# A kernel whose order is written out as numbers: new tables for every engine's order, the dummy products and the PSUM banks

## The chip, the cores and the metric

The kernel runs on one core of a Trainium2 chip. The metric is the device time in microseconds (us) of one execution. Five engines of the core work side by side, each through its own list of instructions in order: TensorE (PE, matrix products; its weight loads are listed as PEld), VectorE (DVE), ScalarE (ACT), GpSimd (POOL) and SyncE (SP, which only issues DMA transfers). They wait for each other by semaphores. Products land in PSUM, which has eight banks.

## The reference

Two parts follow each other: linear attention with second-order features, and a gated feed-forward network on its result.

```python
def phi(x):                       # per head: 32 numbers -> 8 x 8 features
    a = np.einsum('rd,bhsd->bhsr', S1, x)
    b = np.einsum('rd,bhsd->bhsr', S2, x)
    return np.einsum('bhsi,bhsj->bhsij', a, b).reshape(*x.shape[:-1], r * r)
q_p, k_p = (phi(q), phi(k))       # 4 batches, 4 heads, 1088 positions, r = 8
kv = np.einsum('bhsf,bhsd->bhfd', k_p, v)
z = np.sum(k_p, axis=2)
num = np.einsum('bhsf,bhfd->bhsd', q_p, kv)
den = np.einsum('bhsf,bhf->bhs', q_p, z)[..., None] + 1e-06
x = (num / den)                   # heads joined: 4352 tokens x 128
gate = np.maximum(x @ w_gate, 0.0)          # 128 x 1536
return gate * (x @ w_val) @ w_out           # 1536 x 128
```

## The kernel before, in words

**Stages.** For each batch b the keys are loaded, transposed on VectorE (kt1), multiplied by the sketches on TensorE (ksk) and transposed back out of PSUM by VectorE (kt2). From that come z (TensorE), its scaled copy (zc), a product that puts z beside the sketch weights (w, wc), the key features (kphi: POOL, for batch 0 partly VectorE from a PSUM copy kbc that ScalarE makes) and the sum of features times V (kv on TensorE, kve on VectorE). V is cast to FP16 by ScalarE (vc). Queries go the same way: qt1, qsk, qt2, then bw, red, rd and an for the denominator, qphi for the features, a transpose (qtr, qpt), and num and x, which write a column block of x, transposed, to SBUF.

The first 512 tokens of batch 0 have a path of their own to be ready early (class First, names that begin with f): f sk and f t2 for the scores, f aT, f aTe and f csk for the denominator, f bw, f red and f rd (reciprocal), f rx, f rT and f rTe to spread it, f phi (POOL), f tr and f pt for the features, f num and f xd for the result, each for two halves 0 and 1. The second 512 tokens of batch 0 are group "0,4", which goes the way of the others.

**Feed-forward units.** 102 units follow on x. A unit is a block of tokens by a block of w_gate and w_val columns: g and v are the two products (512 columns of PSUM each), relu (ScalarE) evicts g, h (VectorE) multiplies it by v out of PSUM, and o multiplies by w_out, accumulating in a bank over all units of one token block. In 19 units ScalarE copies v out (vcp) and POOL multiplies (hp). oe evicts the sum, st stores it. Units 0 to 5 belong to the first 256 tokens, 6 to 11 to the next, 12 to 23 to group "0,4". Within a token block the first third of the units uses the first third of the weights (wg0, wv0, wo0), and so on.

**Loads.** SP issues most loads in this order: S1 and S2, the second part of k (k01), V of batch 0 in eight pieces (v000 to v013), wo0, wg0, wv0 as raw float32 (ScalarE casts them: cw), q01, and then k, q and v of the later batches. ScalarE issues the first parts of k and q. POOL issues the other weights (wv1, wg2, wg1, wv2, wo1, wo2) as casting transfers, and in between an instruction named gate: a memset of one element of the buffer that k of batch 1 goes to, so that k1 and all that stands behind it on SP waits for POOL to reach it.

**What sets the order.** Each operation is registered with its engine, its name and what it reads. The table START holds a number for each of the 857 operations; they are issued in the order of these numbers, so that the numbers of one engine's operations are that engine's order. BANKS holds, for each of 268 uses of PSUM, the bank or pair of banks. WARM says ahead of which operation how many dummy products are issued: products of a zero tile with itself, into bank 7, that nothing reads. A chain list (RINGS) orders some operations of different engines when the tables are made; it doesn't change.

```python
order = sorted(self.ops, key=lambda o: (START[o.seq] if START else 0, o.seq))
for o in order:
    if o.seq in WARM:
        warm(WARM[o.seq])
    o.fn()
```

Lines of the profile that the text uses: L1015 dummy products, L367 st (the sketches by an identity), L370 ws, L375 wq, L484 and L486 kt1 of batch 0, L491 kt1 of the others, L507 kt2, L537 kbc, L543 kphi, L557 and L561 vc, L310 weight loads by POOL, L316 cw, L385 L, L391 gate, L394 loads of k, L626 f rx, L624 f rd, L631 f rTe, L532 wc, L641 f pt, L695 f phi, L715 f xd, L987 qt1, L793 qt2, L807 red, L811 rd, L916 g and v, L921 relu, L931 h, L944 o.

Of the kernel before, what the change touches and what calls it, by code (L numbers as in the profile page):

```python
# [32 lines left out]
    2, 5, 0, 8, 4, 42, 10, 11, 12, 16, 18, 23, 25, 29, 3, 13, 1, 14, 33, 68, 36, 87, 20, 98, 71,  # L33
    52, 110, 66, 88, 119, 6, 9, 15, 7, 19, 26, 21, 22, 49, 56, 93, 96, 125, 137, 120, 156, 100,
    105, 113, 190, 171, 132, 221, 207, 396, 446, 441, 451, 387, 17, 28, 31, 34, 35, 41, 47, 51,
    74, 79, 39, 50, 40, 44, 54, 72, 46, 32, 53, 73, 80, 81, 83, 85, 90, 163, 160, 170, 178, 191,
    194, 209, 213, 199, 210, 279, 185, 259, 254, 292, 296, 299, 302, 306, 214, 196, 229, 233,
    265, 270, 309, 314, 367, 383, 358, 438, 291, 324, 450, 455, 459, 460, 463, 298, 289, 312,
    320, 364, 373, 429, 433, 540, 577, 345, 473, 509, 516, 594, 599, 605, 608, 612, 27, 24, 30,
    37, 43, 48, 55, 59, 61, 63, 64, 69, 77, 58, 62, 38, 45, 60, 65, 67, 70, 76, 86, 91, 57, 78,  # L40
    82, 92, 97, 75, 89, 94, 109, 117, 84, 95, 102, 99, 108, 104, 106, 112, 115, 129, 157, 198,
    203, 212, 216, 126, 131, 140, 144, 147, 161, 164, 169, 172, 189, 183, 215, 228, 223, 234,
    240, 243, 246, 250, 269, 319, 322, 238, 252, 260, 288, 294, 318, 362, 369, 315, 308, 321,
    326, 332, 354, 363, 372, 378, 401, 420, 470, 479, 395, 405, 412, 418, 454, 475, 522, 530,
    434, 449, 478, 488, 482, 494, 507, 513, 533, 550, 568, 626, 630, 529, 547, 601, 637, 642,
    658, 703, 706, 506, 514, 511, 538, 598, 602, 606, 610, 621, 742, 749, 103, 114, 136, 142,
    176, 122, 128, 149, 154, 184, 101, 107, 116, 123, 200, 111, 121, 118, 135, 205, 152, 158,
    159, 168, 220, 146, 162, 155, 174, 222, 231, 335, 310, 305, 313, 124, 134, 127, 148, 235,
    138, 167, 166, 175, 217, 239, 141, 153, 143, 150, 173, 245, 133, 145, 130, 139, 165, 257,
    151, 177, 193, 197, 226, 258, 195, 206, 204, 218, 261, 268, 287, 284, 295, 301, 232, 241,  # L50
    266, 276, 293, 219, 224, 242, 247, 304, 272, 297, 290, 307, 317, 331, 278, 282, 280, 303,
    323, 337, 273, 277, 274, 283, 349, 300, 316, 256, 264, 333, 351, 375, 458, 381, 436, 592,
    181, 187, 188, 201, 249, 179, 182, 202, 208, 263, 180, 192, 253, 262, 275, 225, 236, 251,
    271, 281, 227, 230, 237, 255, 285, 186, 211, 244, 248, 267, 286, 311, 390, 330, 486, 340,
    328, 336, 344, 352, 385, 327, 341, 343, 348, 393, 342, 350, 353, 359, 394, 347, 356, 380,
    384, 398, 355, 361, 370, 376, 411, 325, 329, 334, 339, 416, 368, 379, 400, 407, 422, 374,
    386, 414, 419, 426, 440, 338, 346, 357, 366, 444, 360, 365, 371, 392, 445, 388, 403, 410,
    415, 447, 408, 413, 423, 428, 464, 469, 582, 671, 490, 596, 404, 409, 402, 421, 489, 431,
    437, 468, 471, 492, 432, 443, 427, 456, 493, 417, 424, 472, 477, 497, 425, 430, 406, 442,
    501, 382, 391, 389, 399, 505, 435, 453, 462, 467, 510, 466, 474, 452, 461, 508, 526, 481,  # L60
    485, 377, 397, 498, 531, 457, 465, 499, 503, 544, 519, 525, 517, 534, 552, 476, 480, 439,
    448, 520, 557, 580, 733, 587, 679, 684, 495, 500, 512, 518, 559, 484, 496, 532, 541, 561,
    483, 491, 502, 523, 564, 487, 504, 524, 528, 572, 539, 551, 562, 566, 578, 537, 546, 543,
    553, 581, 535, 542, 527, 536, 567, 589, 549, 556, 565, 573, 614, 515, 521, 554, 558, 616,
    555, 570, 574, 579, 632, 600, 607, 609, 615, 634, 569, 584, 624, 631, 643, 649, 813, 804,
    676, 741, 548, 560, 576, 585, 651, 545, 563, 583, 591, 654, 603, 613, 611, 620, 655, 586,
    590, 622, 625, 656, 593, 597, 618, 623, 628, 662, 633, 639, 648, 652, 673, 619, 627, 663,
    666, 677, 571, 575, 595, 604, 681, 588, 617, 636, 641, 687, 629, 635, 638, 647, 692, 640,
# [984 lines left out]
```

## Time and profile before

| what | value |
|---|---|
| runs | 101.98, 315.89, 101.86 us; median 101.98 |
| span of the profiled execution (first to last instruction) | 100.1 us |
| instructions | 3180 |
| DMA | 14799 packets, 12.40 MB |
| products of g and v (L916) | 264 |
| products of o (L944) | 408 |
| dummy products (L1015) | 55, busy 5.9 us |
| relu (L921) | 102, 56.3 us busy, 613 ns mean |
| h (L931) | 84, 53.5 us busy, 673 ns mean |
| hp (L936) | 19, 21.7 us busy, 1158 ns mean |

The profiled execution has no time of its own beside its span; the runs' median lies 1.9 us above that span, which holds what comes before the first and after the last instruction. One of the three runs took 315.89 us; it is an outlier, and the median is not affected.

How to read the rows: a row of the timeline is start, duration (both us), engine, line, operation, what is written and read, how many instructions are merged, and in brackets how long the engine had been idle and for what it waited. A row of the stages is from:to, length, then busy time and (count) for PE, PEld, DVE, ACT and POOL, then the granted clock of TensorE, the share of the 16 DMA engines and GB/s. A row of the chain is start, duration, engine and line. SPq is the queue of SP. Ends of matrix products are modelled.

### The profile page before, as it was taken

To read this page: it belongs to the slowest core of one execution; us is meant where nothing else is said; L and a number is where in the kernel's file an instruction comes from. 1 tells how busy PE (TensorE), PEld (TensorE's weight loads), DVE (VectorE), ACT (ScalarE), POOL (GpSimd) and SP (SyncE) were. 2 spreads that over 40 slices of the span, in tenths; PEclk is the share of its full clock that TensorE was granted. 3 is DMA by queue.
4 is the path that set the end of the run, shared out by engine and by line. 5 is a ranking of instruction groups with operands and counts; after the bars stand their busy time and mean duration, and the time that the engine had idled before them with its cause. 6 is when DMAs were issued, how large, how long until landed. Compare 5 with 4: busy or idle time off the path is not lost.

```text
span 100.1 us, 3180 instructions
## 1 busy us (share of the span) xinstructions
PE 94.2 (94%) x1223; PEld 68.3 (68%) x1223; DVE 82.7 (83%) x175; ACT 84.1 (84%) x169; POOL 65.8 (66%) x89
## 2 busy tenths in 40 slices
PE   6999989989999999999999999999999999999950
PEld 6978969848779965557673656765676665688940
DVE  4778779999989998999998689799746879897940
ACT  3445889999799798998999999899999999998730
POOL 6029947898988999999897699935944404001700
PEclk9999999999999999999999999999999999999999
DMA  2988889999930525208664200071217305003331
GB/s 43 370 229 267 146 122 358 339 269 276 342 125 0 111 66 134 45 12 235 165 182 99 60 0 7 1 169 27 52 29 120 78 0 129 2 7 84 99 105 52
DMA packets 14799, 12.40 MB, mean 124 GB/s; under 512 B 8256, under 2 KB 12352, under 8 KB 14784
## 3 DMA queue, kind: packets, MB, share of 16 engines
q1 hardware_dynamic: 13392, 10.70, 38.5%
q0 software_dynamic: 864, 0.79, 5.8%
q10 hardware_dynamic: 528, 0.72, 2.2%
q8 instruction: 9, 0.15, 0.7%
q14 instruction: 6, 0.05, 0.2%
HBM read 9.05 MB, written 2.23 MB: 113 GB/s over the span
## 4 chain that ended last, share of the span: by engine, by line
PE 81%; ACT 6%; POOL 4%; DMA 3%; issue 1%; DVE 1%
PE ps L916 42%; PE ps L944 23%; PE ps L1015 5%; ACT g_sb L921 4%; DMA wg<-in_moe_w_gate_dram 3%; PE ps L848 3%; PE ps L501 2%; PE ps L780 2%; POOL kp L543 2%; PE ps L567 2%; ACT v_sb L925 1%; POOL fqp L695 1%; ACT qpt L840 1%; PE ps L515 1%; POOL wv L310 1%
## 5 line engine op out<-in xcount | busy, mean ns | idle before, releaser
L921 ACT ACTIVATE g_sb<-ps 128x512 f16<-128x512 f32 x102 | 56.3, 613 | 3.9 <-PE ps L916 3.2
L931 DVE TENSOR_TENSOR ht<-g_sb,ps 128x512 f16<-128x512 f16 (+1 forms) x84 | 53.5, 673 | 7.2 <-PE ps L916 5.6
L916 PE MATMUL ps<-xT,wv 128*128 128x512 f16 (+1 forms) x132 | 35.6, 332 | 0.5 <-ACT g_sb L921 0.5
L916 PE MATMUL ps<-xT,wg 128*128 128x512 f16 (+1 forms) x132 | 34.3, 332 | 0.3 <-DMA wg<-in_moe_w_gate_dram 0.3
L944 PEld LDWEIGHTS <-ht 128*128 128x128 f16 x408 | 28.0, 98 | 9.2 <-issue 0.8
L944 PE MATMUL ps<-wo,ht 128*128 128x128 f16 x408 | 33.8, 219 | 0.0
L936 POOL TENSOR_TENSOR ht<-g_sb,v_sb 128x512 f16<-128x512 f16 x19 | 21.7, 1158 | 16.4 <-ACT g_sb L921 14.9
L916 PEld LDWEIGHTS <-wg 128*128 128x128 f16 x132 | 13.6, 115 | 5.9 <-issue 2.2
L543 POOL TENSOR_TENSOR kp<-kab 128x512 f16<-128x512 f32 (+2 forms) x14 | 15.7, 1136 | 2.0 <-DVE kab L507 2.0
L916 PEld LDWEIGHTS <-wv 128*128 128x128 f16 x132 | 13.9, 114 | 3.6 <-issue 1.3
L821 POOL TENSOR_TENSOR qqp<-qan,qabc 128x1024 f16<-128x1024 f32 (+1 forms) x9 | 14.9, 1658 | 0.4
L925 ACT CAST v_sb<-ps 128x512 f16<-128x512 f32 x19 | 11.3, 601 | 0.6 <-PE ps L916 0.5
L1015 PE MATMUL ps<-zero 128*128 128x128 f16 x55 | 5.9, 285 | 1.0 <-DVE zero L292 1.0
L793 DVE STREAM_TRANSPOSE qabc<-ps 128x128 f32<-128x128 f32 (+1 forms) x12 | 5.4, 488 | 1.0 <-PE ps L780 0.6
L987 DVE STREAM_TRANSPOSE qT<-q_sb 128x544 f32<-128x544 f32 (+2 forms) x9 | 5.9, 662 | 0.4 <-DMA q_sb<-in_q_dram 0.4
L1015 PEld LDWEIGHTS <-zero 128*128 128x128 f16 x55 | 5.1, 136 | 1.3 <-DVE zero L292 1.0
L951 ACT ACTIVATE o_sb<-ps 128x512 f32<-128x512 f32 (+1 forms) x10 | 5.2, 521 | 0.7 <-PE ps L944 0.7
L801 POOL TENSOR_TENSOR bw<-qabc 128x128 f32<-128x128 f32 (+1 forms) x9 | 3.7, 412 | 2.9 <-DVE qabc L793 2.9
L815 POOL TENSOR_TENSOR qan<-qabc,qrd 128x128 f32<-128x128 f32 (+1 forms) x9 | 3.3, 372 | 3.3 <-DVE qrd L811 3.3
L861 ACT CAST xT<-ps 128x512 f16<-128x512 f32 (+1 forms) x9 | 4.7, 517 | 0.5 <-PE ps L848 0.5
L491 DVE STREAM_TRANSPOSE kT<-k_sb 128x544 f32<-128x544 f32 x6 | 4.2, 724 | 0.0
L507 DVE STREAM_TRANSPOSE kab<-ps 128x576 f32<-128x576 f32 (+2 forms) x5 | 3.3, 664 | 0.7 <-PE ps L501 0.7
(94 smaller groups left out, 77.4 us busy)
## 6 DMA issues: line engine op xcount, KB each, us to landing
k_sb<-in_k_dram SPq DMA_DIRECT2D x3, 544.0 KB, 6.1
q_sb<-in_q_dram SPq DMA_DIRECT2D x3, 544.0 KB, 4.9
out_dram<-o_sb SPq DMA_DIRECT2D x22, 64.0 KB, 1.7
v<-in_v_dram SPq DMA_DIRECT2D x6, 144.0 KB, 7.7
v<-in_v_dram SPq DMA_DIRECT2D x6, 128.0 KB, 7.6
out_dram<-o_sb SPq DMA_DIRECT2D x16, 32.0 KB, 1.8
v<-in_v_dram SPq DMA_DIRECT2D x6, 64.0 KB, 3.1
k_sb<-in_k_dram SPq DMA_DIRECT2D x1, 288.0 KB, 3.5
```

Source lines behind the costliest of these rows:

```text
L543: eng.tensor_tensor(out=self.kp[:, lo:hi].rearrange("p x g (i a c) -> p (x g i) a c", i=2, a=R), in0=a[:, :, :, None].to_broadcast([128, n ...
L793: nc.vector.transpose(self.abc[:, lo:lo + m, 2 * i2:2 * i2 + 2].rearrange("p x h f -> p h x f"), pair(ls[i2])[:, :, lo * 32:(lo + m) * 32] ...
L821: nc.gpsimd.tensor_tensor(out=self.qp[:, lo:hi].rearrange("p x g (i a c) -> p (x g i) a c", i=2, a=R), in0=self.an[:, lo * H:hi * H, :, No ...
L916: nc.tensor.matmul(bank(l)[:, y * self.W:(y + 1) * self.W], w[:, j // 4, :, j % 4], x, start=True, stop=True, skip_group_check=True)
L921: nc.scalar.activation(out=self.gs, in_=bank(l), func=ACTF.Relu)
L925: nc.scalar.copy(out=self.vs, in_=bank(l))
L931: nc.vector.tensor_tensor(out=self.ht[:, t], in0=self.gs[:, t], in1=bank(l)[:, t], op=ALU.mult)
L936: nc.gpsimd.tensor_tensor(out=self.ht, in0=self.gs, in1=self.vs, op=ALU.mult)
L944: nc.tensor.matmul(o[:, s], self.ht[:, i * 128:(i + 1) * 128], wo[:, j // 4, j % 4], start=(j == 0 and s == 0), stop=(j == NJ - 1), skip_g ...
L951: nc.scalar.mul(out=self.os[:, 0:n * DM], in_=bank(self.lo)[:, 0:n * DM], mul=1.0 / (XSCALE * XSCALE))
L987: nc.vector.transpose(qT[b][:, lo:hi], q_sb[b][:, lo:hi])
L1015: nc.tensor.matmul(PS[:, 7, 0:128], zero, zero, start=True, stop=True, skip_group_check=True)
```

## The change

All three tables are replaced: START (857 numbers), BANKS (268 entries) and WARM. They come from a new search in which the planner holds each load at the landing that was measured for it. No operation is added or removed except dummy products, and each operation stays on its engine; POOL_UNITS, the engine of every load and the chain list are as they were.

```diff
 START = [
-    2, 5, 0, 8, 4, 42, 10, 11, 12, 16, 18, 23, 25, 29, 3, 13, 1, 14, 33, 68, 36, 87, 20, 98, 71,
...
+    1, 4, 2, 8, 5, 44, 11, 12, 13, 15, 17, 26, 29, 31, 3, 18, 0, 20, 37, 90, 40, 93, 22, 49, 84,
...
 ]
 BANKS = [
-    (0,), (2,), (3, 4), (5, 6), (1,), (5,), (3,), (7,), (6, 7), (5,), (2,), (6,), (5, 6), (6,),
...
+    (0,), (3,), (1,2), (1,2), (1,), (6,), (5,), (4,), (0,4), (5,), (6,), (2,), (5,7), (7,), (4,),
...
 ]
-WARM = {34: 29, 63: 2, 143: 14, 147: 1, 152: 9}
+WARM = {34: 19, 61: 2, 63: 2}
```

Read as names, the head of each engine's order changes like this (a number in square brackets is so many dummy products):

```
TensorE before: [29] st, [14] f sk 0, ksk 0 0, [2] ksk 0 4, f aT 1, f aT 0, z 0, sx, [1] f csk 0, f sk 1,
  f csk 1, [9] f rT 0, kv 0 0, w 0, f tr 0, kv 0 2 .. kv 0 8, f rT 1, f tr 1, f num 0, qsk 0,4, g 2, g 0,
  f num 1, g 3, v 2, v 3, g 1, g 6, v 6, v 9, ...
TensorE after:  [19] st, [2] ksk 0 0, f sk 0, f aT 1, [2] ksk 0 4, f aT 0, z 0, f sk 1, sx, kv 0 0, f csk 0,
  f csk 1, f tr 0, kv 0 2, f tr 1, kv 0 4 .. kv 0 8, f rT 0, w 0, f num 0, f rT 1, f num 1, g 0, g 1,
  qsk 0,4, g 7, v 0, v 7, v 9, g 6, g 3, v 1, ...
VectorE before: ..., kt1 0 0, qt1, ws, qt1, kt1 0 4, kt2 0 0, f t2 0, kt2 0 4, kphi 0 2, zc 0, kphi 0 4,
  f bw 0, f red 0, f t2 1, f rd 0, f bw 1, f red 1, f rd 1, kphi 0 6, f rx 1, qt1 0 4, kve 0, f xd 0,
  qt2 x4, red, rd, f xd 1, h 2, red, h 3, rd, h 0, h 6, h 1, kt1 1 1, kt1 1 0, ...
VectorE after:  ..., kt1 0 0, ws, qt1, qt1, kt2 0 0, kt1 0 4, kphi 0 2, f t2 0, kt2 0 4, kphi 0 6, zc 0,
  f t2 1, kphi 0 4, f bw 0, f red 0, f rd 0, f bw 1, f red 1, kve 0, f rd 1, f rx 1, f xd 0, qt1 0 4,
  f xd 1, qt2 x4, h 0, red, h 1, rd, red, h 6, kt1 1 1, kt1 1 0, h 4, ...
ScalarE before: ..., vc 0 1, L, f rx 0, cw g0, f rTe 0, wc 0, f pt 0, cw v0, f rTe 1, f pt 1, cw o0, relu 2, ...
ScalarE after:  ..., cw o0, f aTe 0, vc 0 1, L, f rx 0, f pt 0, f pt 1, f rTe 0, wc 0, cw g0, cw v0, f rTe 1, relu 0, ...
POOL before:    ..., kphi 0 0, kphi 0 8, ld wv1, f phi 0, ld wg2, ld wg1, f phi 1, ld wv2, gate, bw, ld wo1, ld wo2, ...
POOL after:     ..., kphi 0 0, f phi 0, kphi 0 8, f phi 1, ld wv1, ld wg2, ld wg1, ld wv2, gate, ld wo1, ld wo2, bw, ...
SP before:      ..., ld q01, ld k1, ld q1, ld k2, ld v20, ld v12, ld v10, ld v23, ld v11, ld v13, ld v22, ld v21, ld k3, ld q2, ...
SP after:       ..., ld q01, ld k1, ld q1, ld v11, ld v12, ld v10, ld k2, ld v22, ld v23, ld v13, ld q2, ld k3, ...
```

In program order ws (VectorE) stood behind wq (ScalarE), which reads the same PSUM bank; it now stands ahead of it. From there on the order of the 102 units, of the attention work of batches 1 to 3 between them and of the banks differs throughout.

123 rows, old and new, of tables (BANKS, START) are left out of this document.

## The prediction

> **What bounds the kernel now.** I read the page's busy shares first, then the busy time by stage, then the chain that ended last, then the head in order of time. The page alone says TensorE:
>
> ```profile
> PE 94.2 (94%) x1223; PEld 68.3 (68%) x1223; DVE 82.7 (83%) x175; ACT 84.1 (84%) x169; POOL 65.8 (66%) x89
> ```
>
> The table by stage (busy time and count on PE, PEld, DVE, ACT, POOL, then granted clock, DMA share, GB/s) says where it is not:
>
> ```profile
> 5.80:14.58 8.78, 8.43 (x188) 6.67 (x187) 7.04 (x21) 6.29 (x16) 6.31 (x9) 1.00 0.86 198
> 14.58:30.00 15.42, 14.64 (x204) 11.62 (x205) 14.82 (x33) 14.13 (x30) 13.25 (x17) 1.00 0.94 280
> 30.00:96.60 66.60, 66.31 (x795) 45.39 (x792) 57.50 (x107) 61.21 (x120) 44.29 (x43) 1.00 0.30 72
> 96.60:100.10 3.50, 0.00 (x0) 0.00 (x0) 0.00 (x0) 0.38 (x1) 0.00 (x0) 1.00 0.36 103
> ```
>
> Four stages. Up to 14.58 TensorE counts as busy, but with dummy products and small attention products: a chain through all engines sets the pace. From 14.58 to 30 VectorE (14.82 of 15.42) and the DMA engines (share 0.94) are all but full, and TensorE has small holes. From 30 to 96.60 TensorE is the bound, 66.31 of 66.60. The last 3.50 us are one ScalarE eviction and the last store; the span ends at 100.10.
>
> So an order can win in two places only: before 14.58, and in TensorE's holes after it, by these rows 15.42 - 14.64 = 0.78 and 66.60 - 66.31 = 0.29, together 1.1 us. Ends of products are modelled, so the holes may be somewhat larger. The chain that ended last shows what ends the head:
>
> ```profile
> 1.00 3.28 PE ps L1015 x29
> ...
> 11.26 3.28 DMA wg<-in_moe_w_gate_dram
> 14.58 0.63 PE ps L916 x4
> ```
>
> Dummies hold the first score products, and the first feed-forward product (g of unit 2) waits for a gate weight that POOL issued at 11.26.
>
> **The change, part by part.** No operation, load or engine changes, so the work is the same and every price is a shift. I follow the new order engine by engine with the old durations.
>
> *Fewer dummies (55 to 23).* In front of st stand 19 instead of 29. At 3.28/29 = 0.113 us each they end at 1.00 + 2.15 = 3.15 instead of 4.28. VectorE and TensorE around that point, in time order (the row of L367 is st):
>
> ```profile
> 3.58 0.71 DVE L484 STREAM_TRANSPOSE kT<-k_sb 128x512 f32<-128x512 f32 x1
> 4.21 0.61 PE L367 MATMUL ps<-id,s 16*128 16x16 f32 x2
> 5.33 0.19 DVE L370 TENSOR_TENSOR wS<-ps,maskp 128x32 f32<-128x32 f32 x1 [0.70 <-ACT wq L375]
> 5.44 0.43 DVE L987 STREAM_TRANSPOSE qT<-q_sb 128x256 f32<-128x256 f32 x1
> 5.80 0.74 DVE L486 STREAM_TRANSPOSE kT<-k_sb 128x576 f32<-128x576 f32 x1
> 6.78 0.45 DVE L507 STREAM_TRANSPOSE kab<-ps 128x256 f32<-128x256 f32 x1 [0.24 <-PE ps L501]
> ...
> 10.41 0.16 DVE L624 RECIPROCAL frd<-fdn 128x8 f32<-128x8 f32 x1
> ...
> 11.25 0.64 DVE L543 TENSOR_TENSOR kp<-kab,ps 128x512 f16<-128x512 f32 x1
> ```
>
> st can start between 3.15 (dummies) and 4.21 (as now, if the landing of S held it). ws stands ahead of wq now, so it needs st's end and kt1 0 0, which leaves VectorE at 3.58 + 0.71 = 4.29: ws runs at 4.3, at worst 4.8, against 5.33. Both qt1 pieces (0.43 each) follow to 5.2; ksk 0 0 runs beside them with 2 dummies ahead of it instead of 14; kt2 0 0 starts at about 5.3 (at worst 5.8) instead of 6.78.
>
> *VectorE's chain to the reciprocal.* From kt2 0 0 to f rd 0 it took 10.41 - 6.78 = 3.63. The new order puts kt1 0 4 (0.74) and one more kphi (0.64) in between: 5.0 us, so f rd 0 lies near 10.3, at worst 10.8. The gain of 1.5 is spent on moving that work forward. ScalarE meanwhile is held by the last V load:
>
> ```profile
> 9.61 0.73 ACT L561 CAST v<-v 128x640 f16<-128x640 f32 x1 [0.62 <-DMA v<-in_v_dram]
> 10.24 0.26 ACT L385 COPY L<-ps 128x128 f32<-128x128 f32 x1
> 10.61 0.40 ACT L626 COPY frx<-frd 128x256 f32<-128x256 f32 x1
> 11.30 0.62 ACT L316 CAST wg<-qabc 128x512 f16<-128x512 f32 x1 [0.29 <-DMA qabc<-in_moe_w_gate_dram]
> 11.83 0.37 ACT L631 COPY frT<-ps 128x256 f32<-128x256 f32 x1
> 12.15 0.19 ACT L532 COPY wq<-ps 128x32 f32<-128x32 f32 x1
> ...
> 13.64 0.60 ACT L641 COPY fpt<-ps 128x512 f16<-128x512 f16 x1
> ...
> 15.03 2.56 ACT L921 ACTIVATE g_sb<-ps 128x512 f16<-128x512 f32 x5 [0.26 <-PE ps L916]
> ```
>
> *ScalarE's chain to the first product.* SP's order of loads up to q01 is unchanged, so I keep 9.61. The new order is vc 0 1, L, f rx 0, both f pt, f rTe 0, wc 0, cw g0: 0.73 + 0.26 + 0.40 + 0.60 + 0.60 + 0.37 + 0.19 + 0.62 = 3.77, so 13.4 end to end, or 12.7 with each start 0.1 ahead of the end before it, as 9.61 + 0.73 and 10.24 show. I take 13.0. The first product is now g of unit 0, whose raw weight is in SBUF by 11.30, so POOL's weight no longer ends the head: **TensorE's stream starts 1.6 us earlier.** cw v0 and f rTe 1 (0.62 + 0.37, overlapped 0.8) come before the first relu: 13.8 against 15.03.
>
> *VectorE at the handover* is what the next stage runs on:
>
> ```profile
> 14.43 0.91 DVE L793 STREAM_TRANSPOSE qabc<-ps 128x128 f32<-128x128 f32 x4
> ...
> 15.64 0.20 DVE L811 RECIPROCAL qrd<-qdn 128x8 f32<-128x8 f32 x1
> 15.76 0.38 DVE L715 TENSOR_TENSOR xT<-ps,frT 128x256 f16<-128x256 f32 x1
> 16.11 0.69 DVE L931 TENSOR_TENSOR ht<-g_sb,ps 128x512 f16<-128x512 f16 x1
> ...
> 17.66 1.83 DVE L931 TENSOR_TENSOR ht<-g_sb,ps 128x512 f16<-128x512 f16 x3
> ```
>
> f xd 1 follows f rTe 1 at 13.8, then four qt2: 13.8 + 0.38 + 0.91 - 0.1 = 15.0 for the first h, against 16.11. Before, a reduction and a reciprocal (0.20 each, 0.35 overlapped) were done by then; now they follow. VectorE's true lead is 0.75 us. TensorE's larger lead runs into VectorE, so 0.75 is what this stage carries on.
>
> *POOL and the next loads.* f phi 0 and f phi 1 move ahead of four weight loads (wv1, wg2, wg1, wv2), and these go out some 1.4 us later than now:
>
> ```profile
> 8.91 0.72 POOL L310 DMA_DIRECT2D wv<-in_moe_w_val_dram  x1
> ...
> 10.67 1.13 POOL L310 DMA_DIRECT2D wg<-in_moe_w_gate_dram  x2
> 11.80 1.21 POOL L695 TENSOR_TENSOR fqp<-fab 128x512 f16<-128x512 f32 x1
> 12.97 0.59 POOL L310 DMA_DIRECT2D wv<-in_moe_w_val_dram  x1
> 13.56 0.09 POOL L391 MEMSET k_sb<- 1x1 f32 x1
> ```
>
> In VectorE's new order f t2 1 ends about 1.2 ahead of f rd 0's 10.3; f phi 1 takes 1.21 from there, to 10.3, the loads 0.72 + 1.13 + 0.59 = 2.4, so the gate (the memset) is reached at 12.8 instead of 13.56. Behind it SP issues k1, whose first reader is kt1 1 1:
>
> ```profile
> 19.41 1.36 DVE L491 STREAM_TRANSPOSE kT<-k_sb 128x544 f32<-128x544 f32 x2
> DMA to landing us min/median/max: 2.8/4.4/7.0
> ```
>
> VectorE reaches kt1 1 1 at 15.0 + 1.83 (three h) + 0.6 (two reductions, a reciprocal) = 17.4; now it is at 19.41 behind five h. By the last row (of k_sb's loads) k1 lands at 12.9 plus 2.8 to 7.0, 15.7 to 19.9, at the median 17.3. Nothing on VectorE can pass kt1 1 1, h and reductions wait behind it, and TensorE for these; so the landing caps the lead. At 17.4 all 0.75 stays, at 18.2 (19.41 less two h) nothing, at 19.9 it is a loss of 1.7. The DMA engines are full there and the weights are late: I take 17.5 and keep 0.7. Moving k2 behind three v1 loads hides behind six h.
>
> *Banks and the order from 30 on.* TensorE can win 0.3 us there, and an order with more waits could lose without bound. I take 0: each TensorE product there is ready before TensorE is.
>
> **Sum.** Span 100.1 - 0.7 = 99.4. The runs' median, 101.98, lies 1.9 above that span; with the same 1.9, **101.3 us**. Own range 100.4 to 102.3.
>
> **Rivals.**
>
> *A, both places win.* k1 lands in time, the lead of 1.6 us at TensorE is kept and the 1.1 us of holes close: 101.98 - 2.7 = 99.3. For it: VectorE's five h before kt1 1 1 become three, so TensorE is asked for less by then. Against it: VectorE has only 0.75 to give.
>
> *B, k1 decides.* Weights issued later share full DMA engines with k1, which lands between 18.2 and 19.9: a gain of 0 to a loss of 1.7, about 102.5. For it: a DMA share of 0.94 over 15 us. Against it: k1 is issued 0.8 earlier.
>
> *C, the slow array (slower than before).* The dummies tell TensorE's rate:
>
> ```profile
> 4.75 1.21 PE L1015 MATMUL ps<-zero 128*128 128x128 f16 x10
> 5.68 0.50 PE L1015 MATMUL ps<-zero 128*128 128x128 f16 x5
> ...
> 10.41 0.67 PE L1015 MATMUL ps<-zero 128*128 128x128 f16 x9
> ```
>
> The early ones go (3.28 - 1.21)/19 = 0.11 us apart, the later ones (0.67 - 0.50)/4 = 0.04 to 0.07, though the granted clock reads 1.00 throughout. Full rate came at about 5.7, after 4.7 us with next to no idle time. In the new order TensorE idles between 3.15 and 5. If it then needs 4.7 us from 5.3 on, the small products run at half rate till 10: up to 2.3 us of them are late, part of it hidden behind ScalarE's 9.61, so some 1.5 reach the first product: 101.98 - 0.7 + 1.5 = 102.8. If the feed-forward stream too starts slow, 4.7 us at half rate cost up to 2.3 more. It decides from the point where full rate comes after about 8 us; I give it 103.2. For it: no fast dummy stands ahead of 4.7 us of activity. Against it: slow products fill the array and so end the slow state themselves.
>
> [...]
>
> **Chances.** Forecast 0.50, A 0.20, B 0.15, C 0.15. 2% (2.04 us) is about what a measurement of this kernel can tell from no change. Faster by more: A's 0.18 and the forecast's tail 0.05, 0.23. Slower by more: C's 0.07, B's 0.03, and 0.02 for new waits after 30: 0.12. Within: 0.65. The range reaches from A, 99.3, to just past C's middle, 103.4.
>
> **What would show it.** Right: kt2 0 0 near 5.3, the first feed-forward product near 13.0 and not behind a weight of POOL, the first h near 15.0, kt1 1 1 near 17.5, and from 30 on the same full TensorE about 0.7 us earlier. Wrong: score products still at half rate after 8 (C), VectorE idle before kt1 1 1 (B), TensorE waiting in 30 to 90 (a worse order), or the holes between 14 and 30 gone (A).

## The result, and the profile after

The changed kernel takes **108.53 us** (median of four runs, 108.25 to 108.88) against 101.92 of the kernel before in the same set: a ratio of 1.0641, 95% interval 1.0592 to 1.0690. The forecast was 101.3, its range ended at 103.4. The profiled execution of the changed kernel took 108.81 us with a span of 107.0. Some runs of a kernel are disturbed and longer, in e17_last 109.05 us against 105.51 to 106.23: ratios leave them out, and where none is given, too few of a kernel's runs lay together and the median and range of all its runs stand instead. Code lines of the changed kernel are 5 lower than before (g and v are L911, relu L916, h L926, o L939, qt2 L788, kt2 L502, num L843, dummies L1010).

The line of busy time on the page:

```profile
PE 96.6 (90%) x1191; PEld 69.5 (65%) x1191; DVE 83.6 (78%) x175; ACT 83.3 (78%) x169; POOL 65.7 (61%) x89
```

The same work on each engine, in a span 6.9 us longer. The table by stage (from:to, length, busy time and count on PE, PEld, DVE, ACT, POOL, clock, DMA share, GB/s):

```profile
5.80:14.58 8.78, 8.78 (x108) 7.47 (x100) 5.31 (x16) 4.64 (x11) 6.80 (x11) 1.00 0.69 179
14.58:30.00 15.42, 13.34 (x213) 10.83 (x212) 12.32 (x29) 12.93 (x27) 11.57 (x14) 1.00 1.05 245
30.00:60.00 30.00, 27.16 (x384) 18.82 (x353) 26.04 (x52) 24.82 (x51) 23.73 (x23) 1.00 0.45 101
60.00:90.00 30.00, 29.71 (x332) 18.79 (x330) 24.16 (x45) 27.38 (x55) 19.38 (x21) 1.00 0.30 68
90.00:103.60 13.60, 13.45 (x147) 10.56 (x145) 12.07 (x21) 11.21 (x23) 2.31 (x2) 1.00 0.14 35
```

From 14.58 on TensorE stands idle for 2.08 + 2.84 + 0.29 + 0.15 = 5.36 us, against 1.07 before: 4.3 us of new holes. The rest goes with a later start: behind 14.58 stand 83.66 us of busy TensorE time against 80.95 before, work that was still to do there or ran slowly. The head, in order of time, on TensorE:

```profile
5.84 1.22 PE L661 MATMUL ps<-qT,s1r 128*128 128x128 f32 x4
7.92 1.22 PE L661 MATMUL ps<-qT,s1r 128*128 128x128 f32 x4
10.70 1.90 PE L669 MATMUL ps<-zs,faT 128*128 128x32 f32 x8
14.00 1.19 PE L682 MATMUL ps<-id,frx 128*128 128x128 f32 x4
15.49 0.71 PE L682 MATMUL ps<-id,frx 128*128 128x128 f32 x4
16.39 0.63 PE L911 MATMUL ps<-xT,wg 128*128 128x256 f16 x4
```

The two L682 rows are the same four products: 1.19 us, 0.21 from start to start of the last ones, then 0.71 and 0.11. Up to 15.05 us TensorE runs at half rate, and the first feed-forward product starts at 16.39 instead of 14.58. VectorE, ScalarE and POOL follow late:

```profile
12.36 0.20 DVE L619 RECIPROCAL frd<-fdn 128x8 f32<-128x8 f32 x1
18.63 0.65 DVE L926 TENSOR_TENSOR ht<-g_sb,ps 128x512 f16<-128x512 f16 x1
...
15.58 0.63 ACT L311 CAST wg<-qabc 128x512 f16<-128x512 f32 x1
...
8.50 1.07 POOL L690 TENSOR_TENSOR fqp<-fab 128x512 f16<-128x512 f32 x1 [1.44 <-DVE fab L655]
11.51 0.72 POOL L305 DMA_DIRECT2D wv<-in_moe_w_val_dram  x1
13.80 0.09 POOL L386 MEMSET k_sb<- 1x1 f32 x1
```

The holes after the start, from the chain that ended last (start, duration, engine and line):

```profile
13.83 0.07 POOL k_sb L386
...
17.51 10.64 DMA k_sb<-in_k_dram
28.17 0.75 DVE kT L486
...
30.82 0.73 DVE qabc L788
31.57 0.61 ACT g_sb L916
32.20 0.73 DVE qabc L788
32.97 0.30 PE ps L843 x2
```

k2 goes out at 17.51 (14.58 before) and lands at 28.15. Behind it stands a stretch that makes no sense as data flow: the second half of a transpose (qt2, qabc) behind a relu of another unit, and num of group "0,4" behind both. The waits in the timeline:

```profile
24.66 0.38 PE L911 MATMUL ps<-xT,wg 128*128 128x256 f16 x2 [0.84 <-DVE kab L502]
32.97 0.30 PE L843 MATMUL ps<-qpt,bd 128*64 128x256 f16 x2 [1.59 <-DVE qabc L788]
...
32.20 0.72 DVE L788 STREAM_TRANSPOSE qabc<-ps 128x512 f32<-128x512 f32 x1 [0.66 <-ACT g_sb L916]
...
31.57 0.60 ACT L916 ACTIVATE g_sb<-ps 128x512 f16<-128x512 f32 x1 [2.25 <-DVE qabc L788]
```

The g of unit 10 has nothing to do with kab of batch 1, and a relu nothing with qabc. What they share is PSUM. Three shorter waits behind these transposes follow on TensorE:

```profile
44.35 0.38 PE L911 MATMUL ps<-xT,wg 128*128 128x512 f16 x1 [0.16 <-DVE kab L502]
44.95 0.38 PE L911 MATMUL ps<-xT,wg 128*128 128x512 f16 x1 [0.22 <-DVE qabc L788]
62.77 0.38 PE L782 MATMUL ps<-qT,wq 32*32 32x64 f32 x24 [0.19 <-DVE qabc L788]
```

The five together are 3.0 us, more than half of the idle time behind 14.58. The other waits that the timeline marks there are 0.77 us for wq at 29.64, behind the late k2, 0.87 for the transposing transfer of qpt at 42.37, and 0.36 for a copy of v at 22.52.

### The profile page after: what moved, and what is told of

Its sections match the earlier page's. It is cut to its first block, busy times and chain, and to the rows that moved or that the text cites. A ratio compares the mean times of both kernels' runs of the same rounds, so it can differ in the third digit from the quotient of the medians.

```text
span 107.0 us, 3120 instructions
## 1 busy us (share of the span) xinstructions
PE 96.6 (90%) x1191; PEld 69.5 (65%) x1191; DVE 83.6 (78%) x175; ACT 83.3 (78%) x169; POOL 65.7 (61%) x89
## 4 chain that ended last, share of the span: by engine, by line
PE 62%; DMA 16%; DVE 6%; ACT 4%; SPq 3%; POOL 3%; issue 2%; ACTq 0%; DVEq 0%
PE ps L911 34%; PE ps L939 18%; DMA k_sb<-in_k_dram 10%; DMA qpt<-qqp 4%; ACT g_sb L916 3%; DVE qabc L788 3%; SPq L259 2%; DMA s<-in_S_dram 2%; PE ps L661 2%; PE ps L843 2%; PE ps L496 2%; DVE kT L486 1%; POOL wv L305 1%; DVE ht L926 1%; POOL fqp L690 1%
## 5 line engine op out<-in xcount | busy, mean ns | idle before, releaser
L916 ACT ACTIVATE g_sb<-ps 128x512 f16<-128x512 f32 x102 | 55.2, 619 | 6.3 <-PE ps L911 3.6
L926 DVE TENSOR_TENSOR ht<-g_sb,ps 128x512 f16<-128x512 f16 x84 | 53.8, 674 | 7.4 <-PE ps L911 6.1
L911 PE MATMUL ps<-xT,wg 128*128 128x512 f16 (+1 forms) x132 | 34.3, 331 | 1.4 <-DVE kab L502 1.0
L939 PEld LDWEIGHTS <-ht 128*128 128x128 f16 x408 | 28.1, 98 | 10.8 <-issue 1.7
L911 PE MATMUL ps<-xT,wv 128*128 128x512 f16 (+1 forms) x132 | 35.0, 331 | 0.0
L939 PE MATMUL ps<-wo,ht 128*128 128x128 f16 x408 | 34.5, 219 | 0.0
L911 PEld LDWEIGHTS <-wg 128*128 128x128 f16 x132 | 13.7, 114 | 5.4 <-issue 1.8
L911 PEld LDWEIGHTS <-wv 128*128 128x128 f16 x132 | 13.7, 113 | 3.9 <-issue 1.5
L788 DVE STREAM_TRANSPOSE qabc<-ps 128x128 f32<-128x128 f32 (+1 forms) x12 | 5.7, 499 | 2.0 <-ACT g_sb L916 1.2
L843 PE MATMUL ps<-qpt,bd 128*64 128x512 f16 (+1 forms) x16 | 3.0, 372 | 2.5 <-DVE qabc L788 1.6
L502 DVE STREAM_TRANSPOSE kab<-ps 128x576 f32<-128x576 f32 (+2 forms) x5 | 3.3, 654 | 2.4 <-ACT xT L856 1.3
L562 PE MATMUL ps<-v,kp 128*128 128x64 f16 x72 | 4.9, 205 | 0.0
```

What stands on the lines that cost most here:

```text
L788: nc.vector.transpose(self.abc[:, lo:lo + m, 2 * i2:2 * i2 + 2].rearrange("p x h f -> p h x f"), pair(ls[i2])[:, :, lo * 32:(lo + m) * 32] ...
L911: nc.tensor.matmul(bank(l)[:, y * self.W:(y + 1) * self.W], w[:, j // 4, :, j % 4], x, start=True, stop=True, skip_group_check=True)
L916: nc.scalar.activation(out=self.gs, in_=bank(l), func=ACTF.Relu)
L926: nc.vector.tensor_tensor(out=self.ht[:, t], in0=self.gs[:, t], in1=bank(l)[:, t], op=ALU.mult)
L939: nc.tensor.matmul(o[:, s], self.ht[:, i * 128:(i + 1) * 128], wo[:, j // 4, j % 4], start=(j == 0 and s == 0), stop=(j == NJ - 1), skip_g ...
```

## The experiments

The theories, in the order in which they came up (a rival is one of them, set against another). **1**: a slow array until 15 us and a late k2 together. **2**: the slow array alone. **3**: the new order itself is slower at any rate. **4**: it is when the loads go out, POOL's weights above all. **5**: array and loads together; each hides the other. **6**: the banks; a tile over two banks that are not neighbours is ordered against whatever uses the banks between.

The kernel before took 101.98 to 102.44 (medians) beside the changed ones. "Clock" is the first entry of full speed in the trace's record of the granted clock (ahead of it the views print 1.00): 5.79 us in the kernel before, 15.05 in the changed one.

### Dummies and k2

```diff
 # e1_dummies, e4_both: the changed kernel
-WARM = {34: 19, 61: 2, 63: 2}
+WARM = {34: 29, 61: 14, 63: 2, 147: 1}
 # e2_few: the kernel before
-WARM = {34: 29, 63: 2, 143: 14, 147: 1, 152: 9}
+WARM = {34: 19, 143: 2, 63: 2}
 # e3_k2, e4_both: the changed kernel, SP's order
-ld k1, ld q1, ld v11, ld v12, ld v10, ld k2
+ld k1, ld q1, ld k2, ld v11, ld v12, ld v10
```

> The changed kernel (its order and banks), with more dummy products at the start: 29 ahead of st and 14 ahead of ksk 0 0, where the old order had the same numbers ahead of st and of f sk 0. Theory 1 (two causes: the array stays slow until about 15 us because TensorE idles early, and the new order of loads lets k2 land late): full rate from about 6 us, so the f aT products take near 0.6 us for four instead of 1.22, f rd 0 lies near 10.5 instead of 12.36, and the first feed-forward product at 13.0 to 13.7 instead of 16.39; k2 still goes out behind three v1 loads, so some holes stay: 102.5 to 105, middle 103.7. Rival 2 (only the slow array matters): 100.5 to 102. Rival 3 (the new order is slower at any rate of the array, the early start of the stream is given back in holes): 107 to 108.5.

Measured: 110.54 (108.69 to 111.29), clock at 4.25. **All three missed, theory 1 by 3.7 us even in the fastest run.** In the profiled run (110.53) the array was fast (the four products of L661 took 0.71), yet k1 still landed at 20.44 and k2 at 30.19, and TensorE stood 3.35 us in one hole at 28.3. A fast array alone buys nothing here: the fastest run, 108.69, is no faster than the changed kernel.

> The kernel before (its order and banks) with 23 dummy products instead of 55: 19 ahead of st and 2 each ahead of f sk 0 and ksk 0 4. Theory 1: with few dummies the old order has the slow array too, small products take double until 12 us or later, the first feed-forward product moves from 14.58 to 15.5 to 16.5, and the time is 103 to 105. Rival 2 (only the slow array matters): 107 to 108.5, all of the loss. Rival 3 (only the order matters): 101.5 to 102.5, as before.

Measured: 106.46 (104.05 to 107.48). In its profiled run (107.48) the clock came at 19.61. Theory 1's mechanism holds in the old order: the dummies are worth 1.9 us by the best run, 104.05, which lies in theory 1's range; the median lies between that range and rival 2's. In that profile q of batch 0 also landed late (6.41 instead of 4.17), so part of its 5.3 us may be that load.

> The changed kernel with one move: the load of k2 goes out right behind q1 as in the old order, ahead of the three loads of v1, dummies as in the change. Theory 1: k2 is issued near 15 instead of 17.51 and lands near 23 to 25 instead of 28.15, VectorE no longer waits at kt1 2 1 and the holes of TensorE between 25 and 33 shrink by 1 to 2 us: 106.5 to 107.7. Rival 2 (slow array only): 108 to 109, since the holes only move to the v1 loads. Rival 3 (the order as a whole): 107.5 to 109.

Measured: 109.85 (106.62 to 110.00). Inconclusive: k2 landed at 25.32, but in the profiled run of 106.62 the clock came at 9.16 with the same dummies, and which of the two made it faster cannot be told.

> The changed kernel with both edits: 29 and 14 dummy products at the start, and the load of k2 ahead of the three loads of v1. Theory 1: 101 to 102.7, at the level of the kernel before. Rival 2 (slow array only): the same as the dummies alone, 100.5 to 102, k2 adding nothing. Rival 3 (the order as a whole): 106 or more.

Measured: 1.0464 (1.0385 to 1.0544), median 107.94. Theory 1 missed by 4 us: clock at 4.97, yet wg1 landed only at 18.01 and k1 at 21.16, and the holes behind VectorE's transposes stood there as in the changed kernel, 0.83 and 1.59 us by the rows of TensorE (the expectations count them as 1.0 and 1.76). This led to theory 4.

### The loads

```diff
 # e5_wts: the changed kernel, POOL's order
-kphi 0 0, f phi 0, kphi 0 8, f phi 1, ld wv1, ld wg2, ld wg1, ld wv2, gate
+kphi 0 0, kphi 0 8, ld wv1, f phi 0, ld wg2, ld wg1, f phi 1, ld wv2, gate
 # e6_all: the same, with e4's dummies and k2, and wo1, wo2 behind the first bw
 # e7_late: the kernel before, POOL's order
-ld wv1, f phi 0, ld wg2, ld wg1, f phi 1, ld wv2
+f phi 0, f phi 1, ld wv1, ld wg2, ld wg1, ld wv2
 # e8_k2late: the kernel before, SP's order
-ld k2, ld v20, ld v12, ld v10
+ld v20, ld v12, ld v10, ld k2
```

> The changed kernel with POOL's four weight loads put back to their old places (wv1 ahead of f phi 0, then wg2 and wg1, f phi 1, wv2); dummies, k2 and all else as in the change. Theory 4 (new: what counts is when the loads go out; the weights behind f phi 0 and 1 leave the DMA engines idle from 11 to 13 us, and then share them with k1 and q1, so k1, q1, v1, k2 land late): weights out at 8.5 to 11.5, k1 lands near 18.5 to 19.5 instead of 20.70, holes of TensorE between 20 and 35 shrink: 105 to 107. Rival 2 (slow array): 108 to 109. Rival 3 (the new order as a whole): 107.5 to 109.

Measured: 1.0819 (1.0749 to 1.0889). Missed, and slower: k1 did land at 19.16 instead of 20.70, but f phi 1, which TensorE's new order wants early, now stands behind three weights and starts at 12.30 instead of 10.50, and the clock came only at 21.19. Which of the two made it slower is not separated.

> The changed kernel with three parts undone together: POOL's four weight loads in their old places and its two wo loads behind bw, the load of k2 ahead of those of v1, and 46 dummies at the start. Theory 4: loads land as before the change and the array is fast, so the stream starts early and finds its data: 101 to 103.5. Rival 3 (the new order as a whole, waits on VectorE and ScalarE that no load explains): 105 to 108.

Measured: 1.0828 (1.0756 to 1.0901). Missed by 7 us although k1 landed at 17.92 and k2 at 21.68. TensorE's full rate did not last, as the stages of this run show (the granted clock is the third figure from the end):

```profile
7.60:11.00 3.40, 3.01 (x60) 2.42 (x55) 2.79 (x9) 1.88 (x5) 2.44 (x4) 1.00 0.89 261
11.10:14.40 3.30, 1.96 (x23) 1.80 (x23) 0.51 (x4) 1.55 (x3) 2.57 (x5) 0.50 0.86 121
14.50:17.80 3.30, 3.30 (x17) 2.44 (x17) 1.88 (x6) 1.87 (x5) 0.00 (x0) 0.50 1.03 313
17.90:21.20 3.30, 3.30 (x46) 1.85 (x45) 1.66 (x6) 2.27 (x4) 0.73 (x2) 0.50 1.01 325
21.30:25.00 3.70, 3.47 (x41) 3.09 (x38) 2.76 (x7) 3.54 (x7) 3.61 (x7) 1.00 1.08 260
```

The clock fell to 0.50 at 11.03, right after a stretch of small products, and stayed there for 10.24 us, through stretches in which PE counts as busy without a break.

> The kernel before with one part of the change: POOL's loads wv1, wg2 and wg1 behind f phi 1, next to wv2, as in the new order; 55 dummies. Theory 4: weights out near 11 to 13 us, an idle stretch of the DMA engines near 12, wg2 for the first feed-forward product lands near 15, k1 collides with the weights and lands past 19: 103 to 106. Rival 2 (slow array) and rival 3 (the order of TensorE, VectorE and ScalarE): 101.9 to 102.8, since neither is touched.

Measured: 1.0370 (1.0245 to 1.0496), median 106.81. **Theory 4 holds in the old kernel**: three loads moved behind POOL's f phi cost 3.7%, and rivals 2 and 3 are out for it. From the timeline of TensorE and the chain that ended last, in the profiled run (108.30, the longest of the four):

```profile
19.45 1.04 PE L916 MATMUL ps<-xT,wg 128*128 128x256 f16 x4 [5.06 <-DMA wg<-in_moe_w_gate_dram]
```

```profile
13.05 6.35 DMA wg<-in_moe_w_gate_dram
```

A weight that took 3.28 us from issue to landing when issued at 11.26 takes 6.35 when issued at 13.05. k1 (issued at 14.21) and q1 are then on the DMA engines with it; that they are the cause is argued, not shown. In the changed kernel the same load, issued at 12.76, took 5.65. In the hole of 5.06 us the clock fell as well, to 0.50 from 16.52 to 23.34.

> The kernel before with one other part of the change: k2 goes out behind three loads of v (v20, v12, v10) instead of ahead of them; 55 dummies. Theory 4: k2 is issued near 17 and lands near 24 to 26 instead of 21.56; kt2 and the products of batch 2 wait: 102.5 to 104.5. Rivals 2 and 3: 101.9 to 102.5.

Measured: 1.0109 (1.0022 to 1.0197), median 103.86. By the ratio this is theory 4 at its lower end, but the interval reaches down into the rivals' range. In the profiled run (106.20) k2 landed at 26.88 and VectorE's kt1 2 1 waited 1.84 us for it.

### Array and loads together, and the loads in the old kernel

```diff
 # e9_loads, e10_loads_few: the changed kernel
-POOL: s1r, kphi 0 0, f phi 0, kphi 0 8, f phi 1, ld wv1, ld wg2, ld wg1, ld wv2, gate, ld wo1, ld wo2, bw, bw
+POOL: s1r, ld wg1, ld wv1, kphi 0 0, f phi 0, kphi 0 8, f phi 1, ld wg2, ld wv2, gate, bw, ld wo1, ld wo2, bw
-SP: ld k1, ld q1, ld v11, ld v12, ld v10, ld k2
+SP: ld k1, ld q1, ld k2, ld v11, ld v12, ld v10
 # e9_loads alone
-WARM = {34: 19, 61: 2, 63: 2}
+WARM = {34: 29, 61: 14, 63: 2, 147: 1}
 # e11_early: the kernel before
-POOL: s1r, kphi 0 0, kphi 0 8, ld wv1, f phi 0, ld wg2, ld wg1, ...
+POOL: s1r, ld wg1, ld wv1, kphi 0 0, kphi 0 8, f phi 0, ld wg2, ...
```

> The order of the change for TensorE, VectorE and ScalarE, with its two suspected costs taken away together: 46 dummies at the start, and loads that go out early: POOL's wg1 and wv1 right behind s1r, where POOL waits for VectorE anyway, wg2 and wv2 where they are, wo1 and wo2 behind bw, k2 ahead of v1. f phi 0 and 1 stay where the change has them. Theory 5 (loads and slow array together carry most of the loss, and each alone brings the other's stall to light): no wait for wg1 at 16 us, k1 lands near 17.5 to 18.5, the array stays fast: 101.5 to 104. Rival 3 (the order itself is worse): the holes at 24, 30 and 41 us of TensorE stay (1.0, 1.8, 0.8 us) with landings as in the old kernel: 105 to 108.

Measured: 1.0376 (1.0326 to 1.0426). Rival 3's number, not theory 5's: clock at 4.83, k1 at 17.74, k2 at 22.62, near the 18.40 and 21.56 of the kernel before, and still the same two waits on TensorE:

```profile
24.28 0.38 PE L911 MATMUL ps<-xT,wg 128*128 128x256 f16 x2 [0.84 <-DVE kab L502]
31.76 0.30 PE L843 MATMUL ps<-qpt,bd 128*64 128x256 f16 x2 [1.59 <-DVE qabc L788]
```

0.84 and 1.59, to the hundredth what the changed kernel has at 24.66 and 32.97, with k2 landing 5.5 us earlier. So neither late loads nor a slow array makes these two. That pointed to the banks.

> As the run with early loads, but with the change's 23 dummies. Theory 5: the loads are right, the array slow until some point between 9 and 20 us: 1.5 to 5 us longer than with 46 dummies, 104 to 108. Rival 3: the same time as with 46 dummies, 105 to 108, within 1 us.

Measured: 108.96 (106.89 to 109.52). In the profiled run, the fastest, the clock came at 9.62; it cost 0.3 us against the profiled run of e9_loads (106.60), which is rival 3's answer; by the medians the difference is 2.5 us, which is theory 5's. The other three runs are 2 us longer and have no trace here, so this one stays undecided.

> The kernel before with POOL's wg1 and wv1 right behind s1r, where POOL sat idle for 1.5 us, and nothing else. Theory 5: the first feed-forward product no longer waits for its weight, the gate and k1 go out about 1 us earlier, and 101.98 becomes 100.3 to 101.5. Rival 2 and 3 (the loads do not matter): 101.8 to 102.3. Against theory 5: the two loads take the DMA engines from v and q01 between 8 and 12 us, and the head gets later by up to 0.9 us: 102 to 103.

Measured: 1.0067 (1.0031 to 1.0103). Theory 5 missed, and the line against it came closest: the last piece of v landed at 10.11 instead of 9.51, and the first feed-forward product started at 15.45 instead of 14.58. That the two early weights take the DMA engines from v fits this, and was not tested by itself.

### The banks

A tile over two banks is addressed by one slice with a step, from the lower to the upper bank:

```python
def pair(l):
    b0, b1 = l.banks
    return PS[:, b0:b1 + 1:b1 - b0]
```

In the old BANKS all 17 such pairs are neighbours (the renaming of e13_span below parts all 17). The new table has 13 that are not: ksk of batch 1 in banks 0 and 4, qsk of batch 1 in 0 and 6 and in 4 and 7, and so on; 23 times another live use of PSUM lies between the two banks of such a pair: the relu that waits in the rows above reads g of unit 18 in bank 5, between 4 and 7 and between 0 and 6; the num goes to bank 4, between 0 and 6; the waiting g of unit 10 goes to bank 3, between the 0 and 4 of kab's pair.

```diff
 # e13_span: the kernel before; 0 1 2 3 4 5 6 7 become 0 2 4 6 1 3 5 7 throughout
-    (0,), (2,), (3, 4), (5, 6), (1,), (5,), (3,), (7,), (6, 7), ...
+    (0,), (4,), (1, 6), (3, 5), (2,), (3,), (6,), (7,), (5, 7), ...
 # e12_banks: the changed kernel; pairs made neighbours, 73 of 268 uses moved
-    (0,), (3,), (1,2), (1,2), (1,), (6,), (5,), (4,), (0,4), ...
+    (0,), (5,), (1, 2), (1, 2), (1,), (6,), (6,), (4,), (0, 1), ...
 # e14_all: e12's banks with the loads and dummies of e9_loads
```

> The kernel before with its PSUM banks only renamed (0 stays, 1 becomes 2, 2 becomes 4, 3 becomes 6, 4 becomes 1, 5 becomes 3, 6 becomes 5, 7 stays), so that each pair of banks has other banks between; order, loads, dummies and which tile follows which in a bank are unchanged. Theory 6: waits for the banks between appear, at the kab and qabc transposes above all, and the time is 103.5 to 108. Every other theory: 101.8 to 102.5, since a name of a bank costs nothing.

Measured: **1.0504 (1.0478 to 1.0529)**, 107.05 to 107.36 in four runs. Only theory 6 foresaw any change: the order of every engine is the same instruction by instruction, the clock came at 5.06, k1 landed at 18.04 (18.40 before) and k2 at 22.66 (21.56). The groups of the costliest instructions (busy us, mean ns, then idle us of the engine ahead of them and what ended it), renamed:

```profile
L921 ACT ACTIVATE g_sb<-ps 128x512 f16<-128x512 f32 x102 | 57.0, 609 | 7.9 <-PE ps L916 3.3 <-DVE qabc L793 2.3 <-DVE kab L507 1.0
L916 PE MATMUL ps<-xT,wg 128*128 128x512 f16 (+1 forms) x132 | 34.8, 332 | 1.7 <-DVE qabc L793 1.2 <-DVE kab L507 0.4 <-DVE xT L715 0.2
L944 PE MATMUL ps<-wo,ht 128*128 128x128 f16 x408 | 34.0, 219 | 0.8 <-DVE qabc L793 0.6 <-ACT g_sb L921 0.2
```

and in the kernel before:

```profile
L921 ACT ACTIVATE g_sb<-ps 128x512 f16<-128x512 f32 x102 | 56.3, 613 | 3.9 <-PE ps L916 3.2
L916 PE MATMUL ps<-xT,wg 128*128 128x512 f16 (+1 forms) x132 | 34.3, 332 | 0.3 <-DMA wg<-in_moe_w_gate_dram 0.3
L944 PE MATMUL ps<-wo,ht 128*128 128x128 f16 x408 | 33.8, 219 | 0.0
```

Renaming alone adds "<-DVE qabc" and "<-DVE kab" to relu, g and o, none of which reads a transpose. Both directions of the wait show up in the timeline, here with 1.4 us from start to start of two transposes that stand in one row of 1.31 us, at 54.66, in the kernel before:

```profile
58.37 0.72 DVE L793 STREAM_TRANSPOSE qabc<-ps 128x512 f32<-128x512 f32 x1 [0.38 <-PE ps L780]
59.77 0.72 DVE L793 STREAM_TRANSPOSE qabc<-ps 128x512 f32<-128x512 f32 x1 [0.68 <-PE ps L916]
...
59.14 0.81 PE L916 MATMUL ps<-xT,wg 128*128 128x512 f16 x3 [0.68 <-DVE qabc L793]
```

> The changed kernel with other PSUM banks and nothing else: every tile that spans two banks gets two neighbouring ones, as in the old kernel, where the change gave pairs such as 0 and 4 or 0 and 6 (73 of the leases move, order, loads and the 23 dummies are those of the change). Theory 6 (new: one instruction over two banks that are not neighbours is ordered against all that uses the banks between them, so that TensorE and ScalarE wait for transposes of VectorE that they have nothing to do with): TensorE's holes of 1.0 us at the kab transpose of batch 1 and of 1.76 us at the qabc transposes of batch 1 go, slow array and late loads stay: 104 to 106.5. Rival 3 (the order itself): 107.5 to 109. Rival 5 (loads and array alone): 108 to 109.

Measured: 1.0492 (1.0470 to 1.0514), median 107.11 against 108.53 of the changed kernel: 1.4 us, less than theory 6's 2 to 4.5 but outside the rivals' range. The group of relu in the changed kernel, then in e12_banks:

```profile
L916 ACT ACTIVATE g_sb<-ps 128x512 f16<-128x512 f32 x102 | 55.2, 619 | 6.3 <-PE ps L911 3.6 <-DVE qabc L788 2.2
L916 ACT ACTIVATE g_sb<-ps 128x512 f16<-128x512 f32 x102 | 55.1, 616 | 6.5 <-PE ps L911 6.1
```

The waits for qabc and kab are gone, on TensorE all five of them. In the profiled run (108.88, the longest of the four) k2 landed at 29.96, and a hole of 2.04 us at 29.4 stands just ahead of where the longer bank hole stood: there, with late loads, the banks are only the second thing in the way.

> The order of the change with all three suspected costs taken away: neighbouring banks, 46 dummies, and the early loads (wg1 and wv1 behind s1r, k2 ahead of v1, wo1 and wo2 behind bw). With loads and dummies alone it took 106.5. Theory 6: the holes of 1.0, 1.76 and about 1 us go: 102 to 103.8. Rival 3 (the order itself): 105.5 to 107.

Measured: 1.0270 (1.0212 to 1.0328), median 104.65. Against e9_loads, with the same loads and dummies, the banks give 1.9 us by the medians and 1.1 by the ratios, each to the kernel before that ran beside it; the holes behind the transposes are gone, up to one of 0.30 us. The rest missed theory 6's range by 0.85 us.

### The repaired order

```diff
 # e15_tuned, e16_tuned_few: e12's banks, k2 ahead of v1, and
+POOL: s1r, ld wg1, kphi 0 0, f phi 0, kphi 0 8, f phi 1, ld wv1, ld wg2, ld wv2, gate, bw, bw, hp 7, ld wo1, ld wo2
 # e15_tuned
+WARM = {34: 29, 61: 14, 63: 2, 147: 8, 166: 4}
 # e17_last: as e15_tuned, with ld wv1 behind ld wg1, and ld wo1, ld wo2 behind the first qphi
 # e18_wo: as e17_last, with ld wo1 behind gate and ld wo2 behind the second qphi
```

> The run with all three repairs, itself mended in three places that its trace showed: wo1 and wo2 go out behind hp 7 instead of between the two bw (they held the second bw for 1.1 us and made a hole of 1.0 us at 19.4), wv1 back behind f phi 1 (with wg1 it held the last piece of v to 10.4 us), and 8 dummies ahead of f csk 0 and 4 ahead of f tr 0 (the granted clock had fallen to 0.5 from 10.98 to 14.40). Theory 6 with 5 (banks, loads and array are the whole loss): 101.5 to 103.3. Rival 3 (the order keeps a loss of its own): 103.8 to 105.5.

Measured: 1.0168 (1.0089 to 1.0247), median 104.34, the best of the new order, but in rival 3's range, 1 us above theory 6's. From 30 on its stages are again those of the old kernel, which had 29.73 and 30.00 there:

```profile
30.00:60.00 30.00, 29.69 (x434) 20.21 (x432) 27.79 (x56) 27.20 (x56) 27.39 (x27) 1.00 0.47 103
60.00:90.00 30.00, 30.00 (x291) 19.76 (x289) 24.63 (x44) 28.65 (x57) 16.71 (x18) 1.00 0.24 54
```

What is left above 0.5 us are two waits ahead of 30, and both come from where this study put wo1 and wo2: POOL issued them from 18.70 to 19.83, ahead of the qphi that the first one waits for, and the second one waits for wo1 itself.

```profile
21.36 0.40 PE L831 MATMUL ps<-ident,qqp 128*128 128x128 f16 x4 [0.94 <-POOL qqp L816]
27.17 0.61 PE L939 MATMUL ps<-wo,ht 128*128 128x128 f16 x8 [1.57 <-DMA wo<-in_moe_w_out_dram]
```

> The same mended kernel with only the change's 23 dummies: prices the slow array with loads and banks in order. Theory 5: full rate from between 9 and 20 us instead of 4 to 6, 1.5 to 5 us more than with 57 dummies. Rival 3: within 0.7 us of it.

Measured: 1.0564 (1.0495 to 1.0632), median 108.28: with loads and banks in order, 23 dummies instead of 57 cost 3.9%. The clock came at 21.12 instead of 4.83. Theory 5 holds for the dummies.

> The mended kernel once more, with the two holes that the last one showed taken away: wv1 early again beside wg1 (wv1, wg2 and wv2 between 11.0 and 12.1 us met k1 and q1, so that k2 landed at 24.84 instead of 21.82 and TensorE waited 1.7 us at 25.3), and wo1 and wo2 behind the first qphi (ahead of it they made a hole of 1.1 us at 20.1). Theory 6 with 5: 101.3 to 103. Rival 3 (the order keeps a loss of its own): 103.3 to 104.7, as in the two runs before it.

Measured: 1.0358 (1.0252 to 1.0465), median 105.93. Missed. The expectation had put the long hole down to k2; the row above names wo. Moved back further, wo1 landed at 27.07, as in e15_tuned (27.13), and the hole grew to 2.3 us, since TensorE came to it 0.8 us earlier.

> As the last run, with wo1 right behind the gate, where POOL then waits 5 us for VectorE, and wo2 behind the second qphi. The last two runs' longest hole (1.6 us at 25.3, 2.3 us at 24.5) ended with the landing of wo1, and the hole at 20 with a qphi that wo1 and wo2 held up: both from this study's places for them, not from k2 as the last expectation had it. Theory 6 with 5: no hole over 1 us between 15 and 35, 101.5 to 103.3. Rival 3 (the order keeps a loss of its own): 103.4 to 105.5 with new holes elsewhere.

Measured: 1.0581 (1.0532 to 1.0630), median 107.86. Missed, and one wait stands out: no other above 0.5 us stands on TensorE between 6 and 35. It is that of o of unit 4 (by the order) for wo2, which went out at 23.84 and landed at 30.80:

```profile
30.84 0.58 PE L939 MATMUL ps<-wo,ht 128*128 128x128 f16 x4 [4.33 <-DMA wo<-in_moe_w_out_dram]
```

In that hole the clock fell back too, to 0.50 from 28.94 to 35.76. An estimate from these, if nothing else takes the hole's place: without the 4.3 us the run would take 103.5, and without up to 2.5 more (TensorE at half rate from 30.84 to 35.76) 101 to 103.5, about the old kernel's. That was not run.

## Why the prediction was wrong, point by point

**Two places where order can win.** Right as a reading of the old kernel, but it was taken for a bound on what order can do. Order and banks could also lose, and did: 4.3 us of holes after 14.58, and a first feed-forward product 1.8 us later.

**Banks and the order from 30 on: 0.** This is the first step that failed. Its ground was that each TensorE product is ready before TensorE is; that holds for the old tables only. The text named the danger ("an order with more waits could lose without bound") and gave it 0.02. The new bank pairs put waits between engines that share no data: 5.0% in the old kernel by renaming alone (e13_span). In the changed kernel TensorE stands idle for 3.28 us after 30, against 0.29 before, where the prediction had 0; its five waits behind transposes are 3.0 us, 2.2 of them after 30; undoing the pairs gives 1.4 us back alone (e12_banks), and 1.1 to 1.9 with loads and dummies mended (e9_loads to e14_all). The new pairs stand in the change's own lines: a table entry (0,4), read by a slice that steps over three banks, was there to be weighed.

**Fewer dummies, and rival C.** The second failed step. st, ws and kt2 0 0 came when predicted (3.75, 4.43, 5.46). But the argument against C, that "slow products fill the array" and so bring full rate themselves, is wrong: PE counted as busy for 8.78 of 8.78 us up to 14.58 and full rate came only at 15.05. C's mechanism was the right one, with a chance of 0.15 and a price of 1.5 us at the first product; its time, 102.8 to 103.2, fell far short too. That product came at 16.39 in the changed kernel and at 13.96 in e4_both, which has the same order and a fast array: 2.4 us. e16_tuned_few against e15_tuned gives 3.9% for the whole run. The prediction took a busy TensorE for one that comes to full rate. Over all kernels here the split is by dummies: with 46 or more (13 kernels) full rate came between 4.2 and 6.3 us, with 23 (7 kernels) between 9.2 and 21.2. The later dummies of the old table, 10 of them ahead of f csk 0 and f rT 0, may hold what the first ones bring: with 46, two of five kernels of the new order lost full rate again at 11.0 (e6_all, e14_all), and the three with 57, 12 of them ahead of f csk 0 and f tr 0 (e15_tuned, e17_last, e18_wo), did not lose it there.

**VectorE's chain to the reciprocal, ScalarE's chain to the first product.** f rd 0 at 12.36 instead of 10.3, cw g0 at 15.58 instead of 12.4, first h at 18.63 instead of 15.0. In e4_both, with the fast array, they came at 11.32, 13.16 and 16.22: half to three quarters of what the sums missed was TensorE's rate, the rest waits between engines, which a sum along one engine does not see.

**POOL and the loads, and rival B.** The gate came at 13.80, not 12.8, since f phi waits for scores that are late. k1 landed at 20.70: past B's 19.9, so B happened too, on top of C. "Moving k2 behind three v1 loads hides behind six h" failed: issued at 17.51, landed 28.15, 1.15 us of wait on VectorE and everything behind it; alone in the old kernel it costs 1.1%, between 0.2 and 2.0 (e8_k2late). And the weights, 1.8 to 2.9 us later in e7_late, are worth 3.7% alone. The step kept the old kernel's times to landing, 2.8 to 7.0 us, for the new order of loads: k1 took 6.78 us, near the end of them, where the step had 4.6, and k2 took 10.64, past it.

**The parts do not add.** In the old kernel renamed banks cost 5.0%, late weights 3.7%, fewer dummies 1.9 us or more, late k2 1.1%: some 12 us, where the change costs 6.6. That fits stalls that hide each other, and so does that undoing one part alone did not help (e1_dummies) or made it worse (e5_wts).

**What stays open.** Whether the order of the engines, with banks, loads and dummies repaired, keeps a loss of its own. The best version, at 1.0168, waits 0.94 and 1.57 us for places of wo1 and wo2 that this study chose, about its distance from the old kernel; a version without any such wait was not reached, and none here beats the old kernel. Why the same loads land some 2 us apart from run to run (k2 at 28.15 in the changed kernel, at 30.19 in e1_dummies, which has its order of loads) was not tried.

## What to carry to other kernels

Give a tile over several PSUM banks neighbouring banks, or keep the banks between free: in this kernel a strided slice is ordered against what it steps over, at 5.0% in e13_span, and nothing in the source shows it but the numbers. Look for it in the profile as waits between instructions that share no data. And a load's measured landing is no property of the load: when a search holds it fixed, it may move the issue for free on paper and pay in the next traffic (3.28 and 6.35 us for the same weight); the same goes for dummy products, whose gain is a state that the planner does not see.

## What the runs showed of the hardware

- Where TensorE's clock fell back, it stood at 0.50 for 3.41 us (e8_k2late), 6.83 (e7_late) or 10.24 (e6_all). Stretches in which the profile shows it as busy throughout left it slow: 8.78 of 8.78 us in the changed kernel, 3.30 of 3.30 twice in e6_all.
- It fell back in the middle of a run: after 3.35 us of idle time at 28.3 (e1_dummies), after 1.89 us at 27.1 (e8_k2late), and after a stretch with 3.01 busy of 3.40, most of it small products (e6_all).
- A 128 KB weight load took 3.28 us from issue to landing at 11.26 (before) and 6.35 at 13.05 (e7_late); k_sb's 544 KB loads have a median of 9.4 us on the page of the changed kernel and 6.1 on that of the kernel before, at a DMA share of 1.05 and 0.94 from 14.58 to 30.
